# Two transformer layers on one core: who makes the first shifted copy of the bit-trick exponentials

## The chip, the cores and the metric

The kernel runs on one core of a Trainium2 chip. The metric is the device time of one execution in microseconds (us). Before the change it is 1589.96 us, the median of 8 runs (1586.64 to 1595.33).

The engines are named as in the profile: PE (TensorE, matmuls), PEld (its weight loads), DVE (VectorE), ACT (ScalarE), POOL (GpSimd), SP (SyncE, which issues the DMAs). SBUF is the memory on the core that all of them read, PSUM the banks into which PE writes.

## What is computed

Input is `x` of 2048 rows by 512 columns (bf16). Two layers with the same weights follow each other, each an attention block and an MLP block with a residual:

```
x = x + attention(layernorm(x))          # 32 heads of 16 columns, softmax over 2048 keys
x = x + gelu(layernorm(x) @ w1 + b1) @ w2 + b2      # 512 -> 1792 -> 512
(and the same once more)
```

In the attention, scores are `q @ k.T / 4`, `p = softmax(scores)`, and the output is `p @ v`, then `@ wo`. The heads have only 16 columns, so the exponentials of 32 heads x 2048 x 2048 scores per layer are most of the work that is not matmul.

## The kernel before

**Cells.** The unit of attention work is a cell: the scores of one head against one key tile `kt` (128 keys) and 512 queries, which fill one PSUM bank of 128 x 512 f32 (in the last 512 queries, two heads with 256 queries each). There are 4096 cells: 32 heads, 16 key tiles, 4 query chunks, 2 layers. A *pass* takes four heads (`g`) of one query chunk (`seg`), a whole one 64 cells. `passes()` lists them in order. In layer 1 the key tiles 12 to 15 come last of all out of layer 0, so `passes()` begins layer 1 with partial passes over the key tiles 0 to 11: 8 of the first query chunk and `EARLY` of the second one. Their sums are parked in SBUF (`PART`, `PART1`) and added when the passes over the last four key tiles follow.

**Two ways to an exponential.** Most cells go to ACT (`exps`, L1466): one ACTIVATE reads two or three PSUM banks and writes bf16 to the ring `PT`. The key tiles in `KD` (4 of 16 in each layer) may go to DVE instead. `dfirst` (L1283) reads the bank, multiplies, adds and writes a 16-bit integer whose bits are the bf16 of a rough exponential. `dchain` then makes three shifted copies of it: L1344 adds 32 to copy 0 and gives copy 1, L1346 adds 64 to copies 0 and 1 and gives copies 2 and 3. PE multiplies the four copies with four differently weighted `V` (`VC`, weights `VW`) and so averages the error out. Cells are joined in pairs in a buffer `DU` (four of two cells, one of one cell, a late one of two); the two shifted copies are made for the whole buffer, when all of its cells have been read.

**Who reads what.** `pvs` (L1527) multiplies the exponentials with `V`, four side by side in the columns of PE, and sums them in PSUM bank 5. `norm` transposes that bank to `XT` (L741, L743), takes the reciprocal of the row sums (L746), multiplies (L754, on POOL for most groups) into `OTT` and transposes to `OTN` (L759). After that come `wo`, the layer norm (`ln`, `ln_tile`: L581 to L602, the scaling L602 on POOL, then a DMA transpose), `hpair` and `gelu`, `ytile`, and the next layer's projections (`proj`). POOL also makes the masked queries `QP` (L1085) and the weighted `VC` (L1068).

**The order.** Nothing is ordered by hand. `_Sched` runs through the whole kernel at build time with a cost for every operation and a clock for each engine. At each step it picks, among all generators ("threads"), the operation that can start first (ties by priority), writes it to its engine's queue, and puts waits on semaphores where data crosses engines. On the chip each engine then works through its own queue strictly in order, so a wait at the head of a queue holds all that stands behind it. `attach` adds a DVE cell to a group of ACT scores when its bank is due to be free within `TOL`; these matmuls form one group with one set of waits. `filler` puts matmuls without use (L1125) into gaps of PE, to keep its clock up; their output goes to a free bank.

The scheduler of before knows of no conflict between DVE and POOL.

Of the kernel before, what the change touches and what calls it, by code (L numbers as in the profile page):

```python
# [5 lines left out]
ALU = mybir.AluOpType  # L6
# [25 lines left out]
DU = 9  # L32
# [8 lines left out]
PACE = {(1, 2): (0.03, 0.05, 0.36, 0.02), (1, 3): (0.05, 0.07, 0.55, 0.1)}  # L41
JB = 0.64
JS = 0.025
EARLY = 4
KD = ((4, 5, 6, 7), (0, 1, 2, 12))
NKD = 4
TAIL = 10
# [12 lines left out]
COLD = 8  # L60
DPRIO = 9
CPRIO = 8
FPRIO = 1.5
PVP = 2
PTURG = 6
# [9 lines left out]
SHIFT = 32  # L75
# [126 lines left out]
        self.done = False  # L202


LATENCY = {"pe": 0.20, "act": 0.10, "dve": 0.10, "pool": 0.15, "sp": 0.1}


class _Sched:
# [5 lines left out]
    def __init__(self, P):  # L214
        self.P = P
        self.clock = {e: 0.0 for e in P.ENGS}
        self.end = {}
        self.pools = {}
        self.tokens = {}
        self.threads = []  # L220
        self.nseq = 0
        self.mode = "F"
        self.ops = []
        self.stream = []
        self.filler, self.free, self.fills = None, None, set()

    def pool(self, name, slots):
        self.pools[name] = list(slots)
# [66 lines left out]
    def _prio(self, op):  # L295
        return op.prio() if callable(op.prio) else op.prio

    def landed(self, keys):
        return max(self.end.get(self.P.lastw[k], 0.0) if k in self.P.lastw else 1e9 for k in keys)

# [33 lines left out]
    def run(self):  # L334
        while True:
            moved = True
            while moved:
                moved = False
                for th in list(self.threads):
                    if self._advance(th):  # L340
                        moved = True
            self.threads = [t for t in self.threads if not t.done]
            best = {}
            for th in self.threads:
                if th.op is None:
                    continue
                e = th.op.eng
                rdy = self._ready(th.op)
                if rdy is None:
                    continue  # L350
                best.setdefault(e, []).append((th, rdy))
            if not best:
                if self.threads:
                    raise RuntimeError("stuck: %r" % [(t.prio, t.block) for t in self.threads])
                return
            pick = None
            for e, cand in best.items():
                now = self.clock[e]
                nowc = [c for c in cand if c[1] <= now]
                if nowc:  # L360
                    ch = min(nowc, key=lambda c: (self._prio(c[0].op), c[0].seq))
                else:
                    ch = min(cand, key=lambda c: (c[1], self._prio(c[0].op), c[0].seq))
                start = max(now, ch[1])
                stop = start + self._cost(ch[0].op)
                for c in cand:
                    if c[0].op.slack is not None and c is not ch and c[1] + c[0].op.slack < stop:
                        ch = c
                        start = max(now, ch[1])
                        break  # L370
                if pick is None or start < pick[0]:
                    pick = (start, e, ch[0])
            start, e, th = pick
            op = th.op
            th.op = None
            if op.late is not None:
                op.late(op, start)
            if e == "pe":
                mode = self.mode
                self.fill(start, op)  # L380
                if mode != self.mode:
                    start = max(self.clock["pe"], start - SW * (op.mode != self.mode) + SW * (op.mode != mode))
            ev = self.P.group(e, op.fns, op.reads, op.writes, op.sem, op.by)
            cost = self._cost(op)
            if e == "pe":
                self.mode = op.mode
                self.note(start + cost - op.cost, start + cost, op)
            self.ops.append((e, start, cost, op.writes[0] if op.writes else ""))
            self.clock[e] = start + cost
            self.end[ev] = start + cost + op.tail + LATENCY[e]  # L390

# [110 lines left out]
class _Plan:  # L502
# [215 lines left out]
    def norm(self, l, seg, g, b, part, final):  # L718
# [14 lines left out]
        if not final:  # L733
            yield _Op("dve", DV, lambda e: e.tensor_copy(pt, pv), reads=[key], writes=[pk] + over)
            yield ("rel", "pv", b)
            return
        xt = T["XT"]
        if part:
            yield _Op("dve", DV, lambda e: e.tensor_tensor(out=pt, in0=pt, in1=pv, op=ALU.add), reads=[key, pk], writes=[pk])
            yield ("rel", "pv", b)  # L740
            yield _Op("dve", 0.7, lambda e: e.transpose(xt[:, :], pt), reads=[pk], writes=["XT"])  # L741
        else:
            yield _Op("dve", 0.7, lambda e: e.transpose(xt[:, :], pv), reads=[key], writes=["XT"])  # L743
            yield ("rel", "pv", b)
        x3 = xt[:, :].rearrange("p (k c) -> p k c", c=32)
        yield _Op("dve", 0.23, lambda e: e.reciprocal(T["RC"][:, :].rearrange("p (k o) -> p k o", o=1), x3[:, :, 16:17]),  # L746
                  reads=["XT"], writes=["RC"])
        gb, ts = self.heads(seg, g)
        o = gb % 2
        pool = g < 6 and seg[2] == 512  # L750
        nb = w // 32
        for i, t in enumerate(ts):
# [2 lines left out]
                out=o3, in0=x3[:, i * nb:i * nb + nb, 0:16],  # L755
                in1=T["RC"][:, i * nb:i * nb + nb, None].to_broadcast([128, nb, 16]), op=ALU.mult),
                reads=["XT", "RC"], writes=["OTT.%d.%d" % (o, t)])
        if ts[-1] == 1:
            yield _Op("dve", 0.05 + 0.65 * w / 512, lambda e: e.transpose(T["OTN"][:, gb, q0:q0 + w], T["OTT"][:, o, 0:w]),  # L759
                      reads=["OTT.%d.0" % o, "OTT.%d.1" % o],  # L760
                      writes=["OTN.%d.%d" % (gb, t % 4) for t in self.tiles(seg)])
            yield ("give", ("otn", l, seg, gb))

    def heads(self, seg, g):
# [325 lines left out]
    def free(self, now, ahead):  # L1090
        P = self.P
        best = (None, 1e9)
        src = self.source()
        for b in (6, 7, 0, 1, 2, 3, 4, 5) if src else ():
            k = "B.%d" % b
            if k in ahead or b in self.hold or k in P.lastw and not P.reads.get(k) and P.lastw[k] not in self.s.fills:
                continue
# [78 lines left out]
    def join(self, op, d, b, extra, free):  # L1176
        pools = self.s.pools
        if self.open is None:
            self.open = {"du": pools["du"].pop(0), "cells": [], "full": False}
        pair = self.open  # L1180
        pair["cells"].append(d)
        extra.append((d, b, pair, len(pair["cells"]) - 1))
# [98 lines left out]
    def dfirst(self, pair, j, b):  # L1281
        u = self.T["DU"][pair["du"]][:, 0, j, :]
        yield _Op("dve", 0.68, lambda e: e.tensor_scalar(u, self.bank(b), E_SCALE, E_BIAS, op0=ALU.mult, op1=ALU.add),  # L1283
                  reads=["B.%d" % b], writes=["DU.%d.0.%d" % (pair["du"], j)] + self.over(pair["du"]))
        pair["done"] = pair.get("done", 0) + 1
        if b in MISC:
            yield ("rel", "dbank", b)
        else:
            yield from self.slot_done(0)

    def solo(self):
        s = self.s
# [39 lines left out]
    def dchain(self, pair):  # L1332
# [5 lines left out]
        if self.open is pair:  # L1338
# [2 lines left out]
        n = len(cells)  # L1341
        U = T["DU"][du]
        key = [["DU.%d.%d.%d" % (du, i, j) for j in range(n)] for i in range(4)]
        yield _Op("dve", 0.08 + 0.14 * n, lambda e: e.tensor_scalar(U[:, 1, 0:n, :], U[:, 0, 0:n, :], SHIFT, None, op0=ALU.add),  # L1344
                  reads=key[0], writes=key[1])
        yield _Op("dve", 0.08 + 0.28 * n, lambda e: e.tensor_scalar(U[:, 2:4, 0:n, :], U[:, 0:2, 0:n, :], 2 * SHIFT, None, op0=ALU.add),  # L1346
                  reads=key[0] + key[1], writes=key[2] + key[3])
        self.duleft[du] = n
# [211 lines left out]
    def run(self):  # L1560
        s = self.s
        self.phase = {}
        s.pool("misc", MISC)
        s.pool("dbank", [])
        s.route = self.route
        s.pool("pv", [PVB])
        s.pool("s", range(len(SLOTS)))
# [54 lines left out]
```

The softmax here doesn't subtract the row's maximum and nothing guards it: scores larger than these inputs give would overflow.

## Time and profile before

| | |
|---|---|
| median of 8 runs | 1589.96 us |
| the profiled execution | 1594.49 us |
| its span, first to last instruction | 1592.6 us |
| busy: PE, DVE, ACT, POOL | 1431.6, 1352.4, 1547.8, 198.4 us |
| L1466, exponentials on ACT | 1261 + 29 + 25 + 19 instructions into four tiles |
| L1283, cells read from PSUM by DVE | 711 + 96 + 82 = 889 instructions |
| L1344, first shifted copy | 361 + 96 + 41 = 498 instructions |
| L1346, second and third one | 361 + 96 + 41 = 498 instructions |

Busy time is time in which the engine worked on an instruction. A wait is told as "engine and line that waited <- engine and line that ended it". In the groups, `128x1024 uint16<-128x1024 uint16` is what is written and read, and the number after `x` is how many there were; then come the busy time in us and the mean of one in ns. Three figures with slashes are the shortest, the median and the longest in ns.

### The profile page before, as it was taken

What the parts mean: (1) busy time and instruction counts of PE and PEld (TensorE: products, weight loads), DVE (VectorE), ACT (ScalarE), POOL (GpSimd) and SP (SyncE); (2) the same over time, 40 slices, a digit from 0 to 9 for tenths busy, and PEclk for the clock granted to TensorE, in tenths of its full rate; (3) what the DMA queues carried; (4) which work ended last, traced back from release to release, by engine and by line L of the source; (5) the groups of instructions that cost most, each with busy time, mean ns of one, the idle gap of its engine ahead of it and who ended that gap; (6) DMA issues with size and microseconds to landing.
All of it is one profiled execution on the core that took longest, in us unless ns stands there. A gap on an engine that the chain in (4) does not pass through costs nothing.

```text
span 1592.6 us, 42896 instructions
## 1 busy us (share of the span) xinstructions
PE 1431.6 (90%) x18701; PEld 445.7 (28%) x18701; DVE 1352.4 (85%) x2564; ACT 1547.8 (97%) x1393; POOL 198.4 (12%) x250
## 2 busy tenths in 40 slices
PE   8998889999998898989989998888998889998988
PEld 2222222222222222222222222222222222333344
DVE  5689999888897899978798788899878987998984
ACT  7999999999999999999999999999999999999996
POOL 5210012001110201002020020113001000010000
PEclk9999999999999999999999999999999999999999
DMA  5100001241114311143111521001252004312520
GB/s 140 22 2 1 2 14 41 74 133 41 28 47 121 93 41 24 41 131 81 41 28 48 160 54 28 1 1 28 66 163 54 28 15 144 110 35 85 157 82 29
DMA packets 141767, 96.88 MB, mean 61 GB/s; under 512 B 36877, under 2 KB 141582, under 8 KB 141582
## 3 DMA queue, kind: packets, MB, share of 16 engines
q1 hardware_dynamic: 141582, 94.14, 21.3%
q8 instruction: 149, 2.44, 0.6%
q14 instruction: 36, 0.29, 0.1%
HBM read 84.41 MB, written 2.10 MB: 54 GB/s over the span
## 4 chain that ended last, share of the span: by engine, by line
ACT 68%; PE 28%; DVE 2%; POOL 1%; issue 1%; DMA 0%; ACTq 0%; POOLq 0%
ACT pt L1466 61%; PE ps L512 11%; PE ps L1137 9%; PE ps L1527 8%; ACT g L893 3%; ACT v L1466 2%; ACT kt L1466 1%; ACT q L1466 1%; ACT L893 1%; DVE du L1283 1%; PE ps L1125 0%; ACT L1466 0%; DMA xf<-xln 0%; POOL xln L602 0%; POOL rstd L588 0%
## 5 line engine op out<-in xcount | busy, mean ns | idle before, releaser
L1466 ACT ACTIVATE pt<-ps 128x1536 bf16<-128x1536 f32 (+2 forms) x1261 | 1385.0, 1249 | 19.6 <-PE ps L1137 15.2
L1137 PE MATMUL ps<-qp,kt 32*128 32x512 bf16 x4096 | 540.4, 387 | 139.3 <-ACT pt L1466 103.9
L1283 DVE TENSOR_SCALAR du<-ps 128x512 uint16<-128x512 f32 x711 | 480.1, 685 | 99.6 <-PE ps L1137 91.9
L1527 PE MATMUL ps<-pt,v 128*17 128x512 bf16 (+1 forms) x3368 | 435.3, 361 | 2.3 <-ACT pt L1466 0.8
L1527 PE MATMUL ps<-du,vc 128*17 128x512 bf16 (+1 forms) x2394 | 336.2, 361 | 2.4 <-DVE du L1346 1.1
L1137 PEld LDWEIGHTS ps<-qp,kt 32*128 32x128 bf16 x4096 | 140.6, 91 | 686.6 <-ACT pt L1466 302.3
L1346 DVE TENSOR_SCALAR du<-du 128x2048 uint16<-128x2048 uint16 x361 | 246.5, 687 | 2.5
L1085 POOL TENSOR_SCALAR qp<-q,mask 128x512 bf16<-128x512 bf16 (+1 forms) x91 | 65.8, 723 | 1020.8 <-PE ps L1137 1012.0
L512 PE MATMUL ps<-xf,wr 128*32 128x512 bf16 (+1 forms) x2400 | 170.8, 368 | 0.9 <-DMA xf<-xln 0.7
L1527 PE MATMUL ps<-du,v 128*17 128x512 bf16 (+1 forms) x798 | 155.7, 364 | 1.7 <-DVE xt L743 1.0
L1344 DVE TENSOR_SCALAR du<-du 128x1024 uint16<-128x1024 uint16 x361 | 151.0, 429 | 2.0
L1527 PEld LDWEIGHTS ps<-pt,v 128*17 128x17 bf16 x3368 | 112.0, 89 | 114.0 <-issue 73.8
L512 PE MATMUL ps<-wr,g 128*32 128x512 bf16 x1600 | 125.5, 389 | 5.4 <-ACT g L893 5.0
L1527 PEld LDWEIGHTS ps<-du,vc 128*17 128x17 bf16 x2394 | 93.0, 90 | 63.3 <-issue 29.4
L1527 PE MATMUL ps<-dh,vc 128*17 128x512 bf16 (+1 forms) x321 | 91.3, 361 | 0.0
L872 DVE TENSOR_SCALAR g<-ps,hb1t 128x512 bf16<-128x512 f32 (+1 forms) x112 | 79.9, 713 | 13.4 <-PE ps L512 12.4
L1283 DVE TENSOR_SCALAR dh<-ps 128x512 uint16<-128x512 f32 x96 | 65.8, 686 | 11.4 <-PE ps L1137 10.6
L1283 DVE TENSOR_SCALAR kt<-ps 128x512 uint16<-128x512 f32 x82 | 56.2, 685 | 21.0 <-PE ps L1137 20.2
L512 PEld LDWEIGHTS ps<-xf,wr 128*32 128x32 bf16 x2400 | 53.6, 95 | 60.6 <-issue 32.4
L602 POOL TENSOR_SCALAR xln<-x,rstd,nmr 128x512 bf16<-128x512 bf16 x58 | 57.6, 996 | 33.3 <-DMA xf<-xln 22.0
L754 POOL TENSOR_TENSOR ott<-xt,rc 128x256 bf16<-128x256 f32 x42 | 29.4, 701 | 178.7 <-DVE rc L746 178.7
L1125 PE MATMUL ps<-vc 128*32 128x512 bf16 x476 | 51.5, 400 | 0.1
(93 smaller groups left out, 1185.9 us busy)
## 6 DMA issues: line engine op xcount, KB each, us to landing
wr<-in_B_w_dram SPq DMA_DIRECT2D x256, 256.0 KB, 2.9
wr<-in_A_wqkv_dram SPq DMA_DIRECT2D x24, 256.0 KB, 3.1
wr<-in_A_wo_dram SPq DMA_DIRECT2D x18, 256.0 KB, 3.2
out_dram<-x SPq DMA_DIRECT2D x16, 128.0 KB, 2.8
g<-in_A_wqkv_dram SPq DMA_DIRECT2D x3, 512.0 KB, 5.5
x<-in_A_x_dram SPq DMA_DIRECT2D x3, 512.0 KB, 8.3
q<-in_B_w_dram SPq DMA_DIRECT2D x3, 512.0 KB, 3.9
kt<-in_B_w_dram SPq DMA_DIRECT2D x4, 256.0 KB, 3.3
```

The lines of the kernel that those rows point to most:

```text
L512: return [lambda e, a=a: e.matmul(out[32 * a:32 * a + 32, :], lhsT=lhsT[:, 32 * a:32 * a + 32], rhs=rhs, start=start, stop=stop, tile_posi ...
L602: yield _Op(eng, cost, lambda e: e.tensor_scalar(T["XLN"][:, x, :], T["X"][:, t, :], T["RSTD"][:, t:t + 1], T["NMR"][:, t:t + 1], op0=ALU. ...
L872: yield _Op("dve", 0.21 + n / 966, lambda e, fc=fc, pb=pb: e.tensor_scalar(T["G"][:, fc, q], pb, T["HB1T"][:, fc:fc + 1], None, op0=ALU.ad ...
L893: lambda e, g=g: e.activation(out=g, in_=g, func=ACT.Gelu_apprx_tanh), reads=gk, writes=gk, prio=2)
L1085: yield _Op("pool", 0.1 + 0.6 * w / 512, lambda e, s=s, q=q, i=i, t=t, w=w: e.tensor_scalar(T["QP"][:, s, w * i:w * i + w], q, T["MASK"][: ...
L1125: fns.append(lambda e, o=o, w=w, a=a, m=m: e.matmul(o, lhsT=w, rhs=rhs, start=start, stop=start, tile_position=(0, m * a)))
L1137: return (lambda e: e.matmul(o, lhsT=lhsT, rhs=rhs, start=True, stop=True, tile_position=(32 * a, 0)), ["K%d.%d.%d" % (l, gb, kt // 4), "Q ...
L1283: yield _Op("dve", 0.68, lambda e: e.tensor_scalar(u, self.bank(b), E_SCALE, E_BIAS, op0=ALU.mult, op1=ALU.add), reads=["B.%d" % b], write ...
L1344: yield _Op("dve", 0.08 + 0.14 * n, lambda e: e.tensor_scalar(U[:, 1, 0:n, :], U[:, 0, 0:n, :], SHIFT, None, op0=ALU.add), reads=key[0], w ...
L1346: yield _Op("dve", 0.08 + 0.28 * n, lambda e: e.tensor_scalar(U[:, 2:4, 0:n, :], U[:, 0:2, 0:n, :], 2 * SHIFT, None, op0=ALU.add), reads=k ...
L1466: yield _Op("act", 0.065 + 0.4267 * n, lambda e, src=src, dst=dst: e.activation(out=dst, in_=src, func=ACT.Exp, scale=0.25), reads=["B.%d" ...
L1527: op.fns.append(lambda e, o=o, lhsT=q[0][0][m], rhs=q[0][1][:, n * m:n * m + n], a=a, st=st, sp=sp: e.matmul(o, lhsT=lhsT, rhs=rhs, start= ...
```

## The change

- `dfirst` has a second operation: after a cell has been read from PSUM, POOL makes its shifted copy (`tensor_scalar` times 1.0 plus 32), cell by cell, if POOL's planned clock is less than `SPARE` ahead of DVE's. `dchain` waits until these are done, and makes with DVE only the first copies that are left.
- The scheduler models an SBUF port that POOL and some DVE operations (`DU` to `DU`, and `XLN`) share: `unlocked` moves the start of an operation behind one that holds the port, with `HOLD` as margins. An operation of DVE that follows another of these at once is exempt.
- `norm` takes a token for `XT` ahead of its first read of the PSUM bank, and one for each half of `OTT`.
- `EARLY` goes from 4 to 2. Bank 5 is no longer among the banks that a filler may take at any time.

The diff, without the lines that only set up the pools and lists:

```diff
-EARLY = 4
+EARLY = 2
...
+SPARE = 1.0
...
+HOLD = (0.05, 0.13)
...
+    def locking(self, op):
+        w = op.writes[0] if op.writes else ""
+        if op.eng == "pool":
+            return not w.startswith("RSTD")
+        return op.eng == "dve" and (w.startswith("XLN") or w.startswith("DU") and w.split(".")[2] != "0")
+
+    def unlocked(self, op, rdy):
+        if op.eng not in self.locks or not self.locking(op):
+            return rdy
+        now = t = max(rdy, self.clock[op.eng])
+        for a, b in self.locks["pool" if op.eng == "dve" else "dve"]:
+            if a <= t < b and not (op.eng == "dve" and a >= self.fast[0] and t < self.fast[1] + 0.02):
+                t = b
+        return t if t > now else rdy
...
-                best.setdefault(e, []).append((th, rdy))
+                best.setdefault(e, []).append((th, self.unlocked(th.op, rdy)))
...
+            if self.locking(op):
+                self.fast = (start, start + cost) if e == "dve" else self.fast
+                self.locks[e] = self.locks[e][-3:] + [(start + HOLD[0], start + cost - HOLD[1])]
...
         xt = T["XT"]
+        gb, ts = self.heads(seg, g)
+        yield ("acq", "xt")
...
+        if ts[0] == 0:
+            yield ("take", ("ott", o))
...
+        yield ("rel", "xt", 0)
...
+            yield ("rel", "ott", o)
...
-        for b in (6, 7, 0, 1, 2, 3, 4, 5) if src else ():
+        for b in (6, 7, 0, 1, 2, 3, 4) if src else ():
...
     def dfirst(self, pair, j, b):
...
+        mine = self.s.clock["pool"] < self.s.clock["dve"] + SPARE
+        if mine:
+            pair["pool"].add(j)
         pair["done"] = pair.get("done", 0) + 1
         if b in MISC:
             yield ("rel", "dbank", b)
         else:
             yield from self.slot_done(0)
+        if mine:
+            v = self.T["DU"][pair["du"]][:, 1, j, :]
+            yield _Op("pool", 0.65, lambda e: e.tensor_scalar(v, u, 1.0, float(SHIFT), op0=ALU.mult, op1=ALU.add),
+                      reads=["DU.%d.0.%d" % (pair["du"], j)], writes=["DU.%d.1.%d" % (pair["du"], j)])
+            pair["moved"] = pair.get("moved", 0) + 1
...
     def dchain(self, pair):
...
-        yield _Op("dve", 0.08 + 0.14 * n, lambda e: e.tensor_scalar(U[:, 1, 0:n, :], U[:, 0, 0:n, :], SHIFT, None, op0=ALU.add),
-                  reads=key[0], writes=key[1])
+        yield ("cond", lambda: pair.get("moved", 0) == len(pair["pool"]))
+        rest = [j for j in range(n) if j not in pair["pool"]]
+        if rest:
+            lo, hi = rest[0], rest[-1] + 1
+            yield _Op("dve", 0.08 + 0.14 * len(rest), lambda e: e.tensor_scalar(
+                U[:, 1, lo:hi, :], U[:, 0, lo:hi, :], SHIFT, None, op0=ALU.add),
+                reads=[key[0][j] for j in rest], writes=[key[1][j] for j in rest])
         yield _Op("dve", 0.08 + 0.28 * n, lambda e: e.tensor_scalar(U[:, 2:4, 0:n, :], U[:, 0:2, 0:n, :], 2 * SHIFT, None, op0=ALU.add),
                   reads=key[0] + key[1], writes=key[2] + key[3])
```

In the changed kernel's program the lines are L1310 (L1283 of before), L1322 (the new copy on POOL), L1386 (L1346), L1506 (L1466), L1112 (L1085), L624 (L602), L779 (L754).

## Prediction

> **What bounds the kernel now.** I began with the page's span and busy times, then the chain that ended last:
>
> ```profile
> span 1592.6 us, 42896 instructions
> PE 1431.6 (90%) x18701; PEld 445.7 (28%) x18701; DVE 1352.4 (85%) x2564; ACT 1547.8 (97%) x1393; POOL 198.4 (12%) x250
> ACT 68%; PE 28%; DVE 2%; POOL 1%; issue 1%; DMA 0%; ACTq 0%; POOLq 0%
> ```
>
> ACT works in 1547.8 of 1592.6 us and is idle for 44.8. DVE, which the change relieves, is busy for 1352.4 us and stands in the chain for 2%. So a microsecond saved on DVE is worth nothing by itself: it counts if it takes exponentials from ACT, or if ACT waits less. Next, the waits of ACT and the largest ones of PE's loads and matmuls for DVE:
>
> ```profile
> ACT pt L1466 <- PE ps L1137: 15.2, 31, 1.3
> PEld ps L1137 <- DVE du L1283: 89.6, 152, 1.6
> PEld ps L1137 <- DVE du L1344: 31.6, 60, 1.0
> PEld ps L1137 <- DVE du L1346: 28.9, 55, 1.3
> PEld ps L1137 <- DVE kt L1283: 14.8, 25, 1.1
> ```
>
> ACT waited 15.2 us for scores, in 31 waits; with 1.3 for L1527 and 0.4 for the tile kt that is 17 us in the middle of the kernel. The other 28 us of its idle time lie in the start, the end and small joints. PE's score loads waited 200 us for the cell instructions of DVE (these rows and five smaller ones, for dh and kt), yet little of it reached ACT. The chain's pieces at ACT's gaps (around 497, 561, 697, 1229 us) are matmuls of L512, L1527 and L1137 without a break: there PE had too much to do, and DVE was not the cause. Then the groups with shapes kept apart:
>
> ```profile
> L1466 ACT ACTIVATE pt<-ps 128x1024 bf16<-128x1024 f32 x769 | 800.5, 1083 | 9.0 <-PE ps L1137 7.9
> L1466 ACT ACTIVATE pt<-ps 128x1536 bf16<-128x1536 f32 x491 | 741.3, 1510 | 10.6 <-PE ps L1137 7.3 <-PE ps L1527 1.3
> L1344 DVE TENSOR_SCALAR du<-du 128x1024 uint16<-128x1024 uint16 x350 | 148.4, 434 | 2.0
> L1346 DVE TENSOR_SCALAR du<-du 128x2048 uint16<-128x2048 uint16 x350 | 241.4, 694 | 2.5
> ```
>
> A third bank in an ACTIVATE costs 1510 - 1083 = 427 ns. Last, the ends of durations by source line:
>
> ```profile
> L1344 DVE TENSOR_SCALAR du<-du x361: 228/420/1056, 68.7 to 1562.8; 128x1024 uint16<-128x1024 uint16 x175, 128x512 uint16<-128x512 uint16 x6
> L1346 DVE TENSOR_SCALAR du<-du x361: 383/684/1102, 70.2 to 1563.2; 128x2048 uint16<-128x2048 uint16 x175, 128x1024 uint16<-128x1024 uint16 x6
> L602 POOL TENSOR_SCALAR xln<-x,rstd,nmr x58: 757/768/1905, 20.3 to 1518.7; 128x512 bf16<-128x512 bf16 x58
> L1068 POOL TENSOR_SCALAR vc<-v x24: 643/644/963, 30.0 to 954.2; 128x544 bf16<-128x544 bf16 x24
> ```
>
> The long ends are meetings. In the timeline an L754 of POOL runs from 118.42 to 119.35 us; an L1344 begins at 118.80 and takes 0.84 instead of 0.42. From 545.13 two L602 take 2.92 us while DVE's copies run one behind the other. L1283, which reads PSUM, keeps its 685 ns through such meetings.
>
> **The change part by part.** The instructions are counted in the built program; durations are rows.
>
> *ACT.* 904 cells go to DVE instead of 889. Two-bank exponentials go from 793 to 784, three-bank ones from 540 to 541: -9 x 1.083 + 1.510 = -8.2 us. By the banks alone it is 15 x 0.427 = 6.4 us, since records of neighbours overlap and part of the fixed share is hidden. I take -7. All of it lies on the engine that bounds.
>
> *DVE.* L1344 goes entirely: 148.4 + 27.4 + 17.2 + 2.9 = -195.9 us (four forms). 15 more cells read: +10.3. L1346: ten more pairs and five fewer single cells: 10 x 0.694 - 5 x 0.438 = +4.7. EARLY = 2: two parked sums fewer, two copies and two additions at 0.69, so -2.7. DVE's load falls to about 1169 us. Nothing of these 184 us is taken for the total: they lie beside ACT.
>
> *POOL.* All 904 copies are on POOL, so SPARE never refuses. No row has a 16-bit integer on POOL. The nearest is L1068, two constants and one input: 643 ns for 544 columns, 605 for 512; L1085, with a pointer scalar, has a median of 691; L602, meetings included, a mean of 996. I take 650: 588 us, so POOL is at 786 of 1590 us (745 to 1098 by the ends). It would need (1540 - 198)/904 = 1.5 us a copy to become the bound.
>
> *The hand-over.* Before, copies 1 to 3 followed the last read by 0.42 + 0.69 = 1.1 us. Now come a crossing to POOL (0.11 us in the timeline, from L591's end at 630.47 to L602 at 630.58), 0.65 for the last cell, one back (under 0.1, from L588's end at 630.28 to L591 at 630.31) and 0.69: 1.5 us. A buffer is filled every 1593/503 = 3.2 us and there are five, so 0.4 us more is hidden by the ring; without that cover PE waits in L1527, as it did for 14.1 us on L1346. What DVE's new wait holds is the reads of PSUM queued behind L1386; those hold the bank, the next group of scores, and ACT's slot with it.
>
> *The port.* Priced by the meetings: a 420 ns copy that met POOL took 840, a 684 ns one up to 1102, so 0.42 us. If all 503 L1386 met a copy, that is 211 us and DVE stands at 1380, near the 1352 of now; if none, at 1169. The new order puts reads of PSUM beside POOL's copies, so I take a third of it: 70 us, DVE at 1240. The Trainium skill (SBUF, State Buffer, "Who interferes with whom") says that the second one blocks until the first is done; its page Perfetto Trace Analysis, "Optimizing Scalar/DVE Operations", warns that moving work between these two might therefore not help. By that rule taken at its worst each L1386 would wait out a whole copy, 503 x 0.65 = 327 us, and DVE would be at 1496. The row's 0.42 agrees in kind and is smaller. Either way DVE stays below ACT's 1540.
>
> *POOL's queue.* The copies now stand behind L1085, which waited 1012 us in all for PE, L602 (22 us in 18 waits for the transposes, up to 3.5) and L754 (178.7 us for DVE). Most of these waits were POOL parked with nothing else to do. In the new queue copies are put ahead of them; those behind are late if a wait lasts longer than planned. The transposes land in 2.5 us and the plan allows 3.8, so this one errs on the safe side. SP's queue has the same 393 issues.
>
> *EARLY.* Passes over the last four key tiles of layer 1 now begin at cell 2528 instead of 2624. The last projection of V for them stands on PE at cell 2480 (before: 2471). The cover shrinks from 153 cells to 48, at 1593/4096 = 0.389 us from 59 to 19 us. It holds; where it breaks, ACT starves one for one.
>
> *PE.* 45 more products (a DVE cell needs four, an ACT cell one) at 0.361/4 = 4 us, and 104 more fillers (944 to 1048), planned into 161 us of idle time. *The tokens of norm* only put into the plan what the reads and writes of XT and OTT already forced: nothing.
>
> *Sum.* Against the profiled execution's 1594.5: -7 and ACT's idle time as it is, 1587.5. That execution lay 4.5 above the median of the runs, so 1583 against 1589.96, or -0.4%. A comparison can tell about 0.3% (4.8 us) from no change: 1585.2 and 1594.7 are the borders.
>
> **The rivals.**
>
> *Hand-over late* (slower). POOL's copies come later than planned, through its queue or the port, L1386 waits at DVE's head, reads of PSUM come late, PE's group and ACT's slot too. For it: 904 new crossings to POOL and 503 back, each in strict order. Against: DVE has 184 us more room. Price: the 200 us that PE waits for DVE go with 17 us of ACT's, a share of 8.5%. The 211 us of the port give 18 by that share, less the 7 saved: +11, or 1601. It decides against the change from 12 us on ACT, that is 140 us of lateness, 0.28 us for each L1386.
>
> *Eaten.* 3 to 11 us of new idle time on ACT eat the saving: 1586 to 1594, no change.
>
> *More.* DVE's room removes part of ACT's 17 us: 1583 - 17 = 1566 at most. Against it: those gaps show PE full of its own work.
>
> *EARLY's cover breaks.* 30 us instead of 19 would cost 11, giving 1594. The change of words, that POOL does it "when idle", is no rival: the program moves all copies.
>
> **How the numbers follow.** Forecast, ACT's idle time within 5 us of now (1578 to 1588): 0.45, two thirds of it under 1585.2. More: 0.16. Eaten, EARLY included: 0.15. Hand-over late: 0.24. Faster: 0.30 + 0.16 + 0.02 (the lower edge of eaten) = 0.48; slower 0.24; same 0.28. The likeliest case alone spans 1578 to 1588. The range goes down to 1571, half of "more", and up to 1603, just past the rival's price; what it leaves out is about 0.07 below and 0.11 above.
>
> **What would show it.** Right: L1506 some 8 us less in sum, no first copy on DVE, DVE near 1170 to 1250 busy, L1322 at 0.61 to 0.75 us in the median, ACT's waits for PE still 12 to 22 us. Wrong: L1322 over 1 us; DVE's waits for L1322 over 100 us in sum with PE's waits for DVE above 200; ACT's waits above 30 us; a hole on ACT around cell 2528 (some 980 us).

## The result, and the profile after

The changed kernel takes 1595.31 us (median of 24 runs, 1588.61 to 1600.67), the one before 1589.42 in the same comparisons (66 runs, 1585.84 to 1595.33). The ratio is 1.0031 [1.0023, 1.0039]: slower by 5 us (5.9 by the medians), where 7 less than the earlier median of 1589.96 were forecast. The profiled execution took 1595.73 us. First its span, busy times and the shares of the chain that ended last:

```profile
span 1593.9 us, 43660 instructions
PE 1430.2 (90%) x18829; PEld 443.3 (28%) x18829; DVE 1232.3 (77%) x2082; ACT 1540.5 (97%) x1385; POOL 818.7 (51%) x1152
ACT 69%; PE 28%; DVE 2%; issue 1%; POOL 1%; POOLq 0%; ACTq 0%
```

ACT works 7.3 us less, just as forecast, and DVE 120 us less. But the span is 1.3 us longer: ACT's idle time went from 44.8 to 53.4 us. The waits that answer to those of before (waiter <- releaser: us in all, times, longest):

```profile
PEld ps L1164 <- DVE du L1310: 106.7, 180, 1.5
PEld ps L1164 <- DVE du L1386: 46.2, 81, 1.2
DVE du L1386 <- POOL du L1322: 28.7, 42, 1.0
ACT pt L1506 <- PE ps L1164: 19.0, 35, 1.4
DVE dh L1386 <- POOL dh L1322: 4.9, 7, 0.7
ACT pt L1506 <- PE ps L1567: 4.1, 2, 2.1
DVE kt L1386 <- POOL kt L1322: 3.7, 6, 0.7
```

DVE waits 37.3 us for POOL's copies. PE's score loads wait for DVE's cell instructions about as before (191 us with the smaller rows, 200 before), but now more of it for the reads (L1310, 106.7 after 89.6) and less for the copies (46.2 after 31.6 + 28.9). ACT's own waits rose from 15.2 to 19.0 (scores) and from 1.3 to 4.1 (L1567). The groups with shapes kept apart:

```profile
L1506 ACT ACTIVATE pt<-ps 128x1024 bf16<-128x1024 f32 x759 | 792.1, 1087 | 9.2 <-PE ps L1164 8.6
L1506 ACT ACTIVATE pt<-ps 128x1536 bf16<-128x1536 f32 x490 | 740.8, 1512 | 16.0 <-PE ps L1164 10.4 <-PE ps L1567 4.1
L1322 POOL TENSOR_SCALAR du<-du 128x512 uint16<-128x512 uint16 x728 | 503.3, 696 | 494.4 <-DVE du L1310 476.8 <-DVE mv L605 11.7 <-DVE varr L608 1.3
L1386 DVE TENSOR_SCALAR du<-du 128x2048 uint16<-128x2048 uint16 x361 | 265.2, 741 | 30.5 <-POOL du L1322 28.2
```

And the ends of the durations by source line (shortest/median/longest, ns):

```profile
L1386 DVE TENSOR_SCALAR du<-du x367: 364/685/1156, 70.5 to 1557.5; 128x2048 uint16<-128x2048 uint16 x181, 128x1024 uint16<-128x1024 uint16 x3
L1322 POOL TENSOR_SCALAR du<-du x728: 610/618/1128, 66.8 to 1556.7; 128x512 uint16<-128x512 uint16 x182
```

A copy on POOL takes 618 ns in the median, up to 1128 where it meets one of DVE; L1386's longest is 1156. Nothing in these rows is far from the forecast. The loss is in where ACT is idle. All gaps of more than 0.05 us between ACT's instructions, summed by place from the two traces (us):

| | start | middle, beside stretches of half PE clock | rest of the middle | after the last exponential | length of that tail |
|---|---|---|---|---|---|
| before | 7.5 | 9.0 | 11.2 | 8.9 | 24.4 |
| after | 7.9 | 9.8 | 16.1 | 11.6 | 27.0 |

-7.3 of work + 0.4 + 0.8 + 4.9 + 2.6 of tail = +1.4, the span's +1.3. Three of these places can be looked at. One of the new holes, in lines of PE's and then of ACT's timeline (start, length, engine, line; what it waited for in brackets):

```profile
779.68 0.39 PE L1164 MATMUL ps<-qp,kt 32*128 32x512 bf16 x3
780.00 1.05 PE L534 MATMUL ps<-xf,wr 128*32 128x512 bf16 x16
780.98 0.39 PE L1164 MATMUL ps<-qp,kt 32*128 32x512 bf16 x2
781.29 0.61 PE L1567 MATMUL ps<-du,vc 128*17 128x512 bf16 x8
781.73 0.38 PE L1567 MATMUL ps<-pt,v 128*17 128x512 bf16 x1
781.96 0.38 PE L1567 MATMUL ps<-pt,v 128*17 128x512 bf16 x1
```

```profile
778.38 2.00 ACT L1506 ACTIVATE pt<-ps 128x1024 bf16<-128x1024 f32 x2
782.39 1.45 ACT L1506 ACTIVATE pt<-ps 128x1536 bf16<-128x1536 f32 x1 [2.01 <-PE ps L1567]
```

PE works without a break through 16 matmuls of a projection, two scores and the products of DVE cells, while ACT stands 2.01 us. The three scores that ACT needs next were written from 779.68 on, by 780.07. What it waits for, by the bracket, is L1567: the products of `pt`, from 781.73 to 782.34, which empty the part of the ring `PT` that ACT writes next. The new order of PE's queue put the projection and the products of `du` ahead of them, and no wait for DVE or POOL lies in between. The second new hole is of another kind:

```profile
1043.68 0.69 DVE L812 TENSOR_TENSOR x<-x,ps 128x512 bf16<-128x512 bf16 x1 [1.97 <-PE ps L534]
1044.29 0.68 DVE L763 TENSOR_TENSOR kt<-kt,ps 128x512 f32<-128x512 f32 x1
1045.03 0.61 PE L1567 MATMUL ps<-pt,v 128*17 128x512 bf16 x8 [0.48 <-DVE kt L763]
1045.69 3.71 ACT L1506 ACTIVATE pt<-ps 128x1536 bf16<-128x1536 f32 x3 [2.13 <-PE ps L1567]
```

Here the products that empty the ring wait for bank 5, which L763 (the addition of a parked sum) reads. L763 stands in DVE's queue behind L812, which waited 1.97 us for products of `wo`. So the order of DVE's queue has a part in this one, but no copy of POOL has. These two holes are the 4.1 us of ACT's waits for L1567, 2.8 of the 4.9 us that the middle lost. The tail, in PE's timeline:

```profile
1567.94 1.48 PE L534 MATMUL ps<-q,g 128*32 128x512 bf16 x24 [1.46 <-ACT g L920]
1569.23 0.62 PE L534 MATMUL ps<-wr,otn 128*32 128x512 bf16 x8
1569.66 1.48 PE L534 MATMUL ps<-q,g 128*32 128x512 bf16 x24
```

The last `wo` products (`otn`) are cut in pieces between the MLP's (`g`); before, all 16 ran in one piece:

```profile
1568.96 1.05 PE L512 MATMUL ps<-wr,otn 128*32 128x512 bf16 x16 [1.33 <-DVE otn L759]
```

### The profile page after: what moved, and what is told of

It reads as the page before. It is cut to its first block, busy times and chain, and to the rows that moved or that the text cites. A ratio compares the mean times of both kernels' runs of the same rounds, so it can differ in the third digit from the quotient of the medians.

```text
span 1593.9 us, 43660 instructions
## 1 busy us (share of the span) xinstructions
PE 1430.2 (90%) x18829; PEld 443.3 (28%) x18829; DVE 1232.3 (77%) x2082; ACT 1540.5 (97%) x1385; POOL 818.7 (51%) x1152
## 4 chain that ended last, share of the span: by engine, by line
ACT 69%; PE 28%; DVE 2%; issue 1%; POOL 1%; POOLq 0%; ACTq 0%
ACT pt L1506 60%; PE ps L534 11%; PE ps L1164 9%; PE ps L1567 8%; ACT g L920 3%; ACT kt L1506 2%; ACT v L1506 1%; ACT q L1506 1%; PE ps L1152 1%; ACT L920 1%; ACT L1506 1%; DVE du L1310 0%; DVE du L1386 0%; POOL rstd L610 0%; DVE dh L1386 0%
## 5 line engine op out<-in xcount | busy, mean ns | idle before, releaser
L1506 ACT ACTIVATE pt<-ps 128x1024 bf16<-128x1024 f32 (+1 forms) x1250 | 1375.1, 1253 | 25.2 <-PE ps L1164 19.0
L1322 POOL TENSOR_SCALAR du<-du 128x512 uint16<-128x512 uint16 x728 | 503.3, 696 | 494.4 <-DVE du L1310 476.8
L1310 DVE TENSOR_SCALAR du<-ps 128x512 uint16<-128x512 f32 x728 | 491.8, 685 | 138.8 <-PE ps L1164 132.4
L1567 PE MATMUL ps<-pt,v 128*17 128x512 bf16 (+1 forms) x3355 | 450.2, 361 | 2.5 <-DVE dh L1386 0.9
L1567 PE MATMUL ps<-du,vc 128*17 128x512 bf16 (+1 forms) x2427 | 331.7, 363 | 2.7 <-DVE du L1386 2.6
L1386 DVE TENSOR_SCALAR du<-du 128x2048 uint16<-128x2048 uint16 (+1 forms) x367 | 267.8, 736 | 31.0 <-POOL du L1322 28.7
L534 PE MATMUL ps<-xf,wr 128*32 128x512 bf16 (+1 forms) x2400 | 164.9, 370 | 1.3 <-DVE g L899 0.5
L1567 PE MATMUL ps<-du,v 128*17 128x512 bf16 (+1 forms) x809 | 154.9, 365 | 2.1 <-DVE du L1310 1.1
L1567 PEld LDWEIGHTS ps<-pt,v 128*17 128x17 bf16 x3355 | 116.0, 89 | 120.2 <-issue 81.5
L1112 POOL TENSOR_SCALAR qp<-q,mask 128x512 bf16<-128x512 bf16 (+1 forms) x89 | 63.9, 718 | 88.5 <-PE ps L1164 79.1
L1567 PEld LDWEIGHTS ps<-du,vc 128*17 128x17 bf16 x2427 | 91.9, 90 | 58.2 <-issue 27.6
L1322 POOL TENSOR_SCALAR dh<-dh 128x512 uint16<-128x512 uint16 x95 | 72.2, 760 | 63.4 <-DVE dh L1310 61.4
L1567 PE MATMUL ps<-dh,vc 128*17 128x512 bf16 (+1 forms) x318 | 88.6, 358 | 0.0
L1322 POOL TENSOR_SCALAR kt<-kt 128x512 uint16<-128x512 uint16 x81 | 56.7, 703 | 52.1 <-DVE kt L1310 50.5
L1310 DVE TENSOR_SCALAR dh<-ps 128x512 uint16<-128x512 f32 x95 | 65.0, 684 | 13.1 <-PE ps L1164 11.9
L1310 DVE TENSOR_SCALAR kt<-ps 128x512 uint16<-128x512 f32 x81 | 55.3, 683 | 18.5 <-PE ps L1164 17.4
L624 POOL TENSOR_SCALAR xln<-x,rstd,nmr 128x512 bf16<-128x512 bf16 x58 | 55.3, 957 | 6.5 <-DMA xf<-xln 2.9
```

The source lines that it names most:

```text
L534: return [lambda e, a=a: e.matmul(out[32 * a:32 * a + 32, :], lhsT=lhsT[:, 32 * a:32 * a + 32], rhs=rhs, start=start, stop=stop, tile_posi ...
L624: yield _Op(eng, cost, lambda e: e.tensor_scalar(T["XLN"][:, x, :], T["X"][:, t, :], T["RSTD"][:, t:t + 1], T["NMR"][:, t:t + 1], op0=ALU. ...
L1112: yield _Op("pool", 0.1 + 0.6 * w / 512, lambda e, s=s, q=q, i=i, t=t, w=w: e.tensor_scalar(T["QP"][:, s, w * i:w * i + w], q, T["MASK"][: ...
L1322: yield _Op("pool", 0.65, lambda e: e.tensor_scalar(v, u, 1.0, float(SHIFT), op0=ALU.mult, op1=ALU.add), reads=["DU.%d.0.%d" % (pair["du"] ...
L1506: yield _Op("act", 0.065 + 0.4267 * n, lambda e, src=src, dst=dst: e.activation(out=dst, in_=src, func=ACT.Exp, scale=0.25), reads=["B.%d" ...
L1567: op.fns.append(lambda e, o=o, lhsT=q[0][0][m], rhs=q[0][1][:, n * m:n * m + n], a=a, st=st, sp=sp: e.matmul(o, lhsT=lhsT, rhs=rhs, start= ...
```

## The experiments

**Theories.** *New order*: a plan made anew has its own holes on ACT, its own tail and its own stretches of half clock; their change of some us outweighs the 7 us of work. *Hand-over and port*: copies on POOL come late or block DVE, and this reaches ACT. *No worth in the relief*: DVE's time was never worth anything, so that only costs remain. Each comparison below is with the kernel before in the same set of runs; its median differs by up to 1.4 us between the sets, so kernels of different sets are compared by their distance from it. "clock" is the median granted TensorE clock of the runs.

### Are the copies' length and lateness the cost?

`e1_tiny_pool_copy`, the changed kernel:

```diff
-            yield _Op("pool", 0.65, lambda e: e.tensor_scalar(v, u, 1.0, float(SHIFT), ...
+            yield _Op("pool", 0.65, lambda e: e.tensor_scalar(v[:, 0:8], u[:, 0:8], 1.0, float(SHIFT), ...
...
-  U[:, 2:4, 0:n, :], U[:, 0:2, 0:n, :], 2 * SHIFT
+  U[:, 2:4, 0:n, :], U[:, 0:1, 0:n, :].to_broadcast([128, 2, n, 512]), 2 * SHIFT
...
-                self.dq[(pi, a)].append((ws, U[:, i, jj, :].bitcast(BF16), ...
+                self.dq[(pi, a)].append((ws, U[:, 0 if i == 1 else i, jj, :].bitcast(BF16), ...
```

> The changed kernel, every engine's order and every wait as they are, but POOL's copy L1322 covers 8 of 512 columns; the rest of copy 1 is left out, and L1386 and PE read copy 0 in its place. Theory 'lateness' (POOL's copies and the port hold DVE, PE and ACT up): 5 us or more faster than the changed kernel's 1595.3, that is 1590 or less. Theory 'order' (the new order of PE's queue costs the time, whoever copies) and theory 'clock' (more half-clock stretches of PE): 1593 to 1598, ACT's waits for PE as before at 20 to 27 us.

1594.89 us against 1588.81, ratio 1.0041 [1.0029, 1.0054]. The same order with hardly a copy is no faster than with whole ones. Its waits:

```profile
ACT pt L1506 <- PE ps L1164: 16.9, 37, 1.3
DVE du L1386 <- POOL du L1322: 10.0, 32, 0.3
```

L1386's wait fell from 28.7 to 10.0 us and POOL's busy time from 818.7 to 437.7, DVE's from 1232.3 to 1206.4: the meetings cost DVE 26 us. ACT's wait for scores fell by 2.1 us, and the total by nothing that can be told. Its two waits for L1567 are those of the changed kernel (4.1 us). The short copies leave 12.8 of the 37.3 us that L1386 waits for POOL; what they take away of the hand-over and the port is not the cause in this order.

`e2_tiny_first_copy`, the kernel before with its order, L1344 over 8 columns of each cell (and L1346 and PE reading copy 0 for copy 1, as in e1):

```diff
-  U[:, 1, 0:n, :], U[:, 0, 0:n, :], SHIFT
+  U[:, 1, 0:n, 0:8], U[:, 0, 0:n, 0:8], SHIFT
```

> The kernel of before, order and waits kept, but the first shifted copy L1344 covers 8 of 512 columns a cell (the rest of copy 1 left out, copy 0 read in its place): what DVE's relief is worth with no new order and no POOL. My forecast took nothing for it: 1588 to 1591 against 1589.4. If DVE's load were what ACT waits for: 1580 or less.

1588.85 against 1588.81, ratio 1.0001 [0.9992, 1.0010]. DVE's busy time fell by 99 us, to 1253.6, and ACT's wait for scores from 15.2 to 10.4:

```profile
ACT pt L1466 <- PE ps L1137: 10.4, 25, 0.9
```

The total did not move. (The profiled execution of e2 has a clock of 0.992 where that of before has 0.988, so the 4.8 us of wait may not be DVE's doing.) In the order of before, relief of DVE is worth nothing by itself.

### What is a new order worth without the copies?

Five kernels have a new order, and no copy on POOL.

`e3_dve_copies`, the changed kernel with DVE making all copies:

```diff
-SPARE = 1.0
+SPARE = -1e9
```

> The changed kernel with SPARE = -1e9: DVE makes all first copies, the port model, the tokens and EARLY = 2 stay (887 cells on DVE, two-bank exponentials 797, three-bank 538). Theory 'lateness': back to 1589 or less, since no copy is on POOL. Theory 'order': somewhere in 1588 to 1600 by what its own order brings, with the tail and single holes on ACT; theory 'EARLY': slow as the changed kernel, 1595.

`e11_port_model_tokens`, the same with `EARLY` of before, which leaves the port's model, the tokens and bank 5:

```diff
-SPARE = 1.0
+SPARE = -1e9
-EARLY = 2
+EARLY = 4
```

> The changed kernel with DVE making all first copies and EARLY = 4: what is left of the change is the port model and the tokens (887 cells on DVE, two-bank 803, three-bank 534, +1.1 us on ACT). Theory 'port model and tokens cost': 1594 or more, as the changed kernel. Theory 'order': 1588 to 1596. Theory 'EARLY': 1589 to 1590.

`e9_before_early2` and `e17_before_early3`, the kernel before with `EARLY` alone:

```diff
-EARLY = 4
+EARLY = 2
```

(3 in the second one.)

> The kernel of before with EARLY = 2 alone (892 cells on DVE, exponentials of two banks 805, of three 531: about -1 us of ACT's work by the spacing of 0.904 and 1.330 us). Theory 'EARLY' (the shorter cover costs time): 1592 to 1596. Theory 'order': within 4 us of 1588.6 on either side, since every new plan has its own holes.

> The kernel of before with EARLY = 3 alone: 885 cells on DVE (two-bank 795, three-bank 540, +1.8 us of ACT's work). If EARLY = 3 is what makes e14 fast: 1585 or less. Theory 'order': 1589 to 1599, as the other new orders of the kernel of before.

`e10_planner_constant`, the kernel before; only the cost that the planner gives to L1283 moves by 5 ns:

```diff
-        yield _Op("dve", 0.68, lambda e: e.tensor_scalar(u, self.bank(b), E_SCALE, E_BIAS, ...
+        yield _Op("dve", 0.685, lambda e: e.tensor_scalar(u, self.bank(b), E_SCALE, E_BIAS, ...
```

> The kernel of before, with the planner's cost of a read of PSUM at 0.685 in place of 0.68 and nothing else: the same work in another order (883 cells on DVE; two-bank 793, three-bank 542, +2.7 us on ACT). Theory 'order' (a new plan by itself costs time, since the old one was picked for its few holes): 1592 to 1598, with more holes in the middle and a clock under 0.994. If orders are alike: 1591 plus or minus 1.5.

| | DVE cells | us (n) | before | ratio | gaps in the rest of the middle |
|---|---|---|---|---|---|
| e3 | 887 | 1595.38 (5) | 1588.81 | 1.0047 [1.0035, 1.0060] | 16.0 |
| e11 | 887 | 1598.93 (6) | 1589.94 | 1.0065 [1.0045, 1.0084] | 15.5 |
| e9 | 892 | 1598.78 (5) | 1589.94 | 1.0055 [1.0039, 1.0071] | 15.5 |
| e17 | 885 | 1596.42 (5) | 1588.84 | 1.0053 [1.0039, 1.0066] | 13.9 |
| e10 | 883 | 1594.08 (12) | 1589.94 | 1.0024 [1.0013, 1.0035] | 13.2 |

All five are 4.1 to 9.0 us slower than before. Their cells differ from before's 889 by +3 to -6, at 0.427 us each -1.3 to +2.6 us of ACT's work; the rest is order. In e10 six cells more on ACT explain 2.6 of 4.1 us; the other 1.5 us are left to 5 ns in a planner's constant, but the interval (2.1 to 5.6 us) does not tell them from nothing. The other four are clear of it. So the order of before is better than its five neighbours here. This also shows what the copies bring: e11 and e4 (below) differ by the copies alone, 1598.93 and 1593.00; e17 and e18 by all of the change but `EARLY`, 1596.42 and 1588.54; e3 and the changed kernel by the copies, 1595.38 and 1595.31. The differences, by the distances from before -4.8, -7.9 and -0.7 us, have the scatter of the orders in them.

Two of these kernels missed what was expected of a mere new order: e9 (at most 1592.6) and e11 (at most 1596). e11 is as slow as expected if the port's model and the tokens cost time; e9 and e17, which have neither, are 8.8 and 7.6 us slower than before as well, so that such a cost is not needed, but a share of the two in e3 and e11 is not excluded.

### The rest of the change with the copies

`e4_early4` and `e18_after_early3`, the changed kernel with `EARLY` alone:

```diff
-EARLY = 2
+EARLY = 4
```

(3 in the second one.)

> The changed kernel with EARLY = 4 (904 cells on DVE as well). Theory 'EARLY' (the shorter cover costs time): 1589 or less. Theory 'lateness': unchanged at 1595 within 3 us. Theory 'order': another order, so anything within 1588 to 1600, explained by the tail after the last exponential and by holes on ACT. Theory 'clock': the time follows the granted clock by about 1.05 us for each 0.001, in all four kernels.

> The changed kernel with EARLY = 3 and nothing else: 904 cells (two-bank 777, three-bank 546), 6.5 us less ACT work than before. Theory 'order': 1586 to 1596. If EARLY = 3 is good by itself: 1588 or less, 5 us or more under EARLY = 4 (1593.0) and EARLY = 2 (1595.3).

e4: 1593.00 us (7 runs) against 1588.81, 1.0025 [1.0014, 1.0036], with 904 cells. e18: 1588.54 (11) against 1588.84, 1.0001 [0.9990, 1.0011], with 904 cells, a tail of 24.2 us instead of 27.0, and a clock of 0.991 instead of 0.989. The same 904 cells take 1595.3, 1593.0 or 1588.5 us by the order. `EARLY` has no steady effect: in the kernel before 4 is better than 3 by 7.6 us, here 3 is better than 4 by 4.5.

### The tail, and the clock

`e5_tail_order`, the changed kernel; the `wo` products of the last query chunk get a higher priority:

```diff
-  prio=MID if h else FPRIO
+  prio=0.9 if (l, seg) == (NL - 1, self.segs[l][-1]) else MID if h else FPRIO
```

> The changed kernel, but in the last segment the matmuls of wo have priority 0.9, so that PE doesn't put the MLP's second matmuls between them; cells and copies as in the changed kernel. Theory 'order': the tail after the last exponential goes from 27.0 back to 24.4 us and the time falls by 2 to 3 us, to 1592.5 to 1593.5. Theory 'clock' alone: no change, 1595.

1592.27 us (12 runs) against 1588.59, 1.0025 [1.0014, 1.0036]: 3.7 us above before where the changed kernel is 5.9 above, so 2.2 less, and 2.1 are the tail's (24.9 us instead of 27.0). Its last products of `wo` run whole, behind only 8 of the MLP's:

```profile
1563.49 0.61 PE L534 MATMUL ps<-q,g 128*32 128x512 bf16 x8 [1.46 <-ACT g L920]
1563.92 1.05 PE L534 MATMUL ps<-wr,otn 128*32 128x512 bf16 x16
1564.79 2.35 PE L534 MATMUL ps<-q,g 128*32 128x512 bf16 x40
```

The granted clock differs between executions and between the two kernels, and this has to be known to read the numbers: the runs of before have 0.994 in the median, those of the changed kernel 0.989. Windows of the changed kernel show what lies in it (us; busy time and instructions of PE, PEld, DVE, ACT, POOL; clock; DMA share; GB/s):

```profile
808.00:817.00 9.00, 7.64 (x59) 1.79 (x59) 6.60 (x13) 7.68 (x7) 6.96 (x7) 0.62 0.05 10
1006.00:1019.00 13.00, 11.77 (x102) 2.70 (x102) 9.07 (x16) 10.51 (x10) 5.68 (x10) 0.61 0.00 0
776.00:784.00 8.00, 7.22 (x102) 2.11 (x95) 5.12 (x8) 5.99 (x7) 1.85 (x3) 1.00 0.23 68
```

The clock is 1.00 nearly everywhere, as around the hole at 781, and 0.5 in a few stretches of 3.41 us or a multiple (0.62 and 0.61 are their share of the windows). In the first two windows ACT is idle for 1.3 and 2.5 us. Two kernels tested whether more fillers help.

`e6_before_more_fill`, the kernel before with the same order of all other work, 1624 fillers instead of 964:

```diff
-WARM = 0.38
+WARM = 0.48
```

> The kernel of before with WARM = 0.48: the same order on every engine, but 1624 fillers on PE in place of 964. Theory 'clock': the granted clock rises from about 0.994 to 0.997 or more and the time falls by 2 to 4 us, to 1585 to 1587. If fillers cost as much as the clock gives: 1588 to 1590 at a higher clock.

`e7_after_more_fill`, the changed kernel, each filler's matmul twice, 1068 more of them:

```diff
-            ev = self.P.group("pe", op.fns, op.reads, op.writes)
+            ev = self.P.group("pe", op.fns * 2, op.reads, op.writes)
```

> The changed kernel with every filler's matmuls issued twice (2136 in place of 1068), all orders and waits as they are. Theory 'clock': the clock rises from 0.989 to 0.993 or more, the time falls by 3 to 5 us to 1590 to 1592. Theory 'order' alone: no gain, or up to 3 us slower, since the doubled fillers don't fit the gaps that were planned for one.

e6: 1587.86 us (12 runs) against 1588.59, 0.9999 [0.9989, 1.0008]; the clock rose to 0.996. e7: 1594.43 (5) against 1588.59, 1.0039 [1.0027, 1.0052]; clock 0.998. The busy times of e7:

```profile
PE 1469.8 (92%) x19897; PEld 468.5 (29%) x19897; DVE 1231.6 (77%) x2082; ACT 1542.2 (97%) x1385; POOL 817.7 (51%) x1152
```

and its waits for scores:

```profile
ACT pt L1506 <- PE ps L1164: 12.7, 34, 0.9
```

In e7 the time at half clock went from 37.5 to 6.8 us, and ACT's gaps beside it from 9.8 to 1.8. But the start lost 2.4, the rest of the middle 2.6 and ACT worked 1.7 more. Both forecasts of a gain missed. A higher clock that is bought with matmuls cost about what it brought: e7 lies 5.8 us above before, the changed kernel 5.9.

### The port's model

`e8_pool_copies_only`, the changed kernel without the port's model and the tokens, with `EARLY` of before. Without the tokens two normalisations may be ordered into one another, so that some groups read another group's `XT`; the instructions are the same.

```diff
-        if op.eng not in self.locks or not self.locking(op):
+        if True:
             return rdy
...
-        yield ("acq", "xt")
...
-EARLY = 2
+EARLY = 4
```

> POOL makes the first copies, but the scheduler has no port model, norm takes no tokens and EARLY is 4: 933 cells on DVE, two-bank exponentials 800, three-bank 521, so ACT has some 20 us less work than before. Theory 'the rest of the change costs': 1572 to 1582. Theory 'lateness' (without the port model the copies collide): 1590 or more. Theory 'order and clock': between, 1578 to 1590, with a clock at or under 0.99.

1588.92 us (12 runs) against 1588.59, 1.0000 [0.9987, 1.0014]. The plan now gives DVE 933 cells and ACT works only 1530.0 us, 17.8 less than before; all of it is eaten (21.0 us of gaps in the rest of the middle, 34.1 us at half clock, a tail of 27.0).

`e12_no_port_model_early4_tail` keeps the tokens and has e5's tail; `e13_no_port_model_tiny_copy` is e12 with e1's copies of 8 columns.

```diff
-        if op.eng not in self.locks or not self.locking(op):
+        if True:
             return rdy
...
-EARLY = 2
+EARLY = 4
...
+  prio=0.9 if (l, seg) == (NL - 1, self.segs[l][-1]) else MID if h else FPRIO
```

> POOL's copies and the tokens stay, the port model is off, EARLY = 4, and wo has priority in the tail: 931 cells on DVE, two-bank 814, three-bank 512, so ACT has 18 us less work than before and 11 us less than the changed kernel. If holes and tail are like the changed kernel's without the tail's 2.6: 1582. Theory 'port' (unplanned meetings hold up DVE and through it ACT): 1588 or more, with more DVE waits for L1322 than 37 us.

> The kernel of e12, every order and wait kept, but POOL's copy covers 8 of 512 columns (the rest of copy 1 left out, copy 0 read in its place). Without the port model POOL and DVE meet unplanned. Theory 'port': 1584 or less against e12's 1589.5, since the meetings are gone, and fewer holes in the middle than its 22 us. Theory 'order': 1587 to 1591, the holes come from PE's queue and stay.

e12: 1589.55 us (12 runs) against 1589.94, 0.9994 [0.9982, 1.0007]. e13: 1578.87 (6) against 1589.08, 0.9934 [0.9914, 0.9954]. Here the copies' length costs some 10 us (10.7 by the medians, 9.8 by the distances from before), in one and the same order, where it cost nothing in the changed kernel's. The waits of e12:

```profile
DVE du L1386 <- POOL du L1322: 28.8, 41, 1.1
ACT pt L1506 <- PE ps L1164: 20.5, 49, 1.1
```

and of e13:

```profile
DVE du L1386 <- POOL du L1322: 9.6, 29, 0.6
ACT pt L1506 <- PE ps L1164: 12.2, 32, 1.3
```

ACT's wait for scores fell by 8.3 us with DVE's wait for POOL. DVE was busy for 1262.0 and 1228.1 us. So the rival is real in an order that plans DVE tighter, with 931 cells; the short copies relieve the hand-over and the port together, and which of them it was is not told apart. It is not what made the changed kernel slow.

### Versions that are faster

`e14_early3_no_port_model` is e12 with `EARLY = 3` (936 cells). `e15_port_model_early3` and `e16_port_model_early4` keep the port's model, have e5's tail and a planner's cost nearer to the 618 ns that the trace shows (926 and 922 cells):

```diff
-            yield _Op("pool", 0.65, ...
+            yield _Op("pool", 0.62, ...
-EARLY = 2
+EARLY = 3
...
+  prio=0.9 if (l, seg) == (NL - 1, self.segs[l][-1]) else MID if h else FPRIO
```

(4 in e16.)

> As e12 but EARLY = 3: 936 cells on DVE (two-bank 824, three-bank 504), 20 us less ACT work than before by the spacing of 0.904 and 1.330 us. Theory 'order': half or more of it is lost in holes and half-clock stretches, 1581 to 1592. If only the work counted: 1569 to 1571.

> The changed kernel with EARLY = 3, the planner's cost of POOL's copy at 0.62 in place of 0.65 and wo first in the tail: 926 cells (818 and 511), 16 us less ACT work than before. Theory 'order': 1583 to 1594. If the port model makes better orders than none: under e14 although it has 4 us more ACT work.

> As e15 with EARLY = 4: 922 cells (834 and 502), 14 us less ACT work than before. Theory 'order': 1584 to 1595, apart from e15 by up to 5 us on either side with no reason in the work. If only the work counted: 2 us above e15.

| | us (n) | before | ratio | clock | ACT gaps: half clock, rest |
|---|---|---|---|---|---|
| e14 | 1578.40 (6) | 1589.08 | 0.9931 [0.9910, 0.9952] | 0.992 | 4.9, 18.5 |
| e15 | 1583.12 (10) | 1589.08 | 0.9958 [0.9944, 0.9972] | 0.993 | 3.7, 18.7 |
| e16 | 1588.53 (12) | 1589.08 | 0.9994 [0.9980, 1.0008] | 0.9905 | 9.1, 19.3 |

e14 beats both kernels. Its span and busy times, and from its waits those of ACT for scores:

```profile
span 1577.4 us, 43877 instructions
PE 1422.3 (90%) x18897; PEld 445.3 (28%) x18897; DVE 1259.3 (80%) x2134; ACT 1529.2 (97%) x1387; POOL 850.1 (54%) x1185
```

```profile
ACT pt L1506 <- PE ps L1164: 16.1, 43, 1.0
```

ACT works 18.6 us less than before and is idle for 48.2 instead of 44.8: 15.2 us less span in the profiled executions, 10.7 by the medians. It came out below the range that was expected (1581 to 1592). The changed kernel had the copies on POOL too; it lacked a plan that moves as many cells (904 against 936, 11.3 us of ACT's work), and an order that gives less away (53.4 us of idle time against 48.2). Between e14 and e12 only `EARLY` differs, and the time by some 10 us.

## Why the prediction was wrong

The terms of work held: ACT -7.3 (forecast -7), no first copy on DVE, POOL at 819 (786), L1322 at 0.618 us in the median (0.61 to 0.75), no hole on ACT around cell 2528, at some 980 us. The busy times of L1506's groups fell only by 4.2 us in sum, not 8: two-bank ones took 1087 ns instead of 1083 and three-bank ones 1512 instead of 1510. That DVE came out at 1232 (forecast 1240) is luck: with short copies, nearly free of meetings, it stands at 1206, not 1169, mainly since neighbouring records overlap (before, those of DVE add up to 1498 us where it is busy for 1352), so that taking L1344 out frees less than its 195.9 us; and the meetings cost 26, not 70. The two errors cancel.

The sum missed the median by 12.3 us, and two of its steps carry that.

**"ACT's idle time as it is."** This failed: 53.4 us instead of 44.8, which with the other terms puts the profiled execution 8.2 us above the 1587.5 of the sum. The prediction looked at the new order as moves of the instructions that the change touches, and priced those. But the scheduler decides at every step from its clocks, so every queue was new: 4.9 us of gaps in the middle, with projections and products ahead of those that empty ACT's ring (781 us) and a late bank 5 (1044 us), and 2.6 in the tail, where e5 gives back 2.1 by one priority. The five new orders without POOL's copies lie 4.1 to 9.0 us above the one of before, so such a penalty doesn't need the copies. The rival "Eaten", which had new idle time of this size but no reason for it, was given 0.15 and a price of 3 to 11 us; the 8.6 of new idle time lie inside. Nor was the old idle time as fixed as it was taken to be: two of the four gaps that the prediction put down to PE having too much to do (497 and 697 us) lie in stretches at half clock (496.4 to 499.8, 694.3 to 697.8).

**"That execution lay 4.5 above the median of the runs, so 1583."** This failed too. The offset is no property of the profiler, to be carried over: before's profiled execution had a granted clock of 0.988 where its runs have 0.994, and the changed kernel's had 0.988 where its runs have 0.989, so it lies only 0.4 above its median. 8.2 + 4.5 - 0.4 = 12.3. At an equal clock the two executions are 1.2 us apart; the medians are 5.9 apart, and the runs of the new order spend more time at half clock, by the median clocks 2 x 0.011 x 1594 = 35 us instead of 2 x 0.006 x 1594 = 19. The 104 more fillers, which the prediction let pass as planned into idle time, did not prevent that. That the lower clock is the reason for the difference is not shown: e3 and e10 have a clock of 0.994 and 0.995, as high as before, and are 6.6 and 4.1 us slower all the same.

**The hand-over** was priced at 0.4 us, hidden by the ring. L1386 waited 37.3 us in 55 waits, a mean of 0.68, and e1 shows that nothing of it reached the total. The rival "Hand-over late", with its share of 8.5%, was the wrong reading for this kernel, though not for e12. **The port**: 70 us were taken, and e1 shows 26; the rule that the second one waits for the first to finish (the Trainium skill, SBUF, State Buffer, "Who interferes with whom") agrees in kind, but at its worst it made 327 us, which no run came near.

What stays open: which feature of an order makes the holes and the half-clock stretches. At the stretches themselves the traces show what comes first. Each of the 15 whole ones (8 before, 7 after) begins right behind 3.41 us in which PE was busy for only 1.26 to 2.13 us, in ten of them mostly waiting for ACT, and the gaps of ACT that the table puts beside the stretches lie in the stretch or behind it. The holes at 781 and 1044 us lie at full clock.

## What to carry to other kernels

Where a planner writes the order, an edit's price has two parts: the work it moves, and a new draw of the order; here the draw was worth some 10 us between two settings and the work 7. Measure the draw by a change that should do nothing (another constant, 5 ns of a cost) before you judge the edit, try several settings around it, and never compare the edit with the best order alone. Before an offset between a profiled execution and the runs is carried to another kernel, look at the granted clock of both.

## What the runs showed of the hardware

**The clock.** All whole stretches at half clock in the profiled executions of both kernels last 3.41, 6.83 or 10.24 us, 37.5 us in each. The Trainium skill (TensorE: Matmul & The Clock Gate, Part 1) gives a window of 3413 ns in which PE's activity is watched, and the rows agree. It says that an idle window brings the half clock. Here the 3.41 us ahead of each of the 15 stretches were not idle, but PE was busy in 37 to 62% of them; an exact border does not come out, since after 51% (from 1119.9 us in the changed kernel) the clock stayed at 1.00. Over the changed kernel's runs, 0.001 of mean clock goes with 1.05 us of time (correlation -0.94). Yet fillers that raised the clock from 0.989 to 0.998 saved 0.9 us at most, where 9 would follow from that slope: they cost elsewhere what they saved at the stretches.

**The port.** The instructions of DVE that read PSUM are not touched by POOL (L1310 takes 0.691 us in the median, whether POOL works beside it or not). Those from SBUF to SBUF are, and not only the copies: L779 with two inputs (128x256) took up to 780 ns, 424 in the median, and at most 427 beside the short copies of e1. A 16-bit multiply and add with two constants over 512 columns on POOL takes 0.62 us alone, and 0.99 in the median where it overlaps an L1386; with 8 columns it takes 0.20. DVE made the same copy, two cells at a time, in 0.43, so POOL is the slower of the two by nearly three times for each cell.
